# Spreading the change of layer in an attention and two-layer feed-forward kernel: sums asked for earlier, one weight pair split a step sooner, products read ahead of weight work, stores issued by ScalarE

## The chip, the cores and the metric

The kernel runs on one core of a Trainium2 chip. The metric is the device time of one execution in microseconds (us). Three runs of the kernel before gave 1114.27, 1115.67 and 1118.46 us, a median of 1115.67 us. One more execution was profiled; it took 1115.52 us and its span, from the first to the last instruction, is 1113.7 us. All rows below come from that execution.

## What is computed

Attention over 4 batches, 8 heads, 576 positions and head size 64, with a threshold: of each row of scores only those within tau of the row's maximum are kept. Its output, 2304 tokens by 512, goes through two feed-forward layers:

```python
scores = scale * q @ k.T
scores = where(scores >= max(scores) - tau, scores, -1e9)
x = softmax(scores) @ v                       # 2304 x 512 after the heads are put side by side
h = x @ w_in                                  # layer 0: 512 -> 2048
x = (h * tanh(softplus(h))) @ w_out           #          2048 -> 512
out = ((x @ w_a) * (x @ w_b)) @ w_out2        # layer 1: 512 -> 1536, two matrices, -> 512
```

The weights arrive as 64-bit floating point numbers, the rest as 32-bit ones.

## The kernel before

**Stages.** Attention fills the first 280 us. Then the two layers run as one pipeline of 42 steps (`pipeline`, L542). Layer 0 has steps 0 to 23, three passes of eight; layer 1 has steps 24 to 41, three passes of six. A pass covers 768 tokens as two column blocks of 384; a step covers 256 hidden columns. Step 24 is the first of layer 1; the change of layer is the stretch around it.

**Splitting.** Each matrix product is done as three matmuls in a reduced 32-bit form: an operand becomes a high part (a ScalarE copy that rounds, L171 and L282) and a low part (a VectorE subtraction, L172 and L286).

**Seven products.** All passes but the first of layer 0 use a scheme of seven products for a two-by-two block product, in place of eight. It needs sums of input blocks (`prepare`, `sums`, L276: four VectorE subtractions named `t1`, `t2`, `b01`, `t4` by what they write) and sums of weight blocks (`in_weights`, L212). Where a layer 1 step names a weight sum, it is `wsa` or `wsb`, the split weights are `wia` and `wib` (`wii` in layer 0, `woo` and `wop` for the second matrix).

**Gaps.** A product and all that is emitted behind it is a gap: 7 gaps in a layer 0 step, 14 in a layer 1 step (7 for `w_a`, 7 for `w_b`), 8 in the first pass. In each gap the program emits, in this order: the product on TensorE (`product`, L338); whatever earlier gaps had put off to this one (`later`), which includes the sums and splits of the next pass's input; one stage of the weights' conversion (`narrow_some`); the share of weight work (`next(fed)`, L572: sums and splits of a later step's weights); then `after` (L384), which reads the product out of PSUM; last the second matmuls of the step before (`second`, L434). Engines run their instructions in the order in which they are emitted.

**Two banks.** The seven products of a step share PSUM tiles with `bufs=2`, so a product may start only when the reads of the product before it in the same bank are done: product 3 needs the VectorE addition `u2` that reads product 1 (L397), product 5 needs `u3`, the next step's product 1 needs `c12` (L415) of this step's product 6.

**Conversion.** `narrow` (L92) turns 64-bit weights into 32-bit ones in scratch memory: a load of `raw`, four gaps of waiting, then on VectorE L106, L107, L115 and L117 and on ScalarE L105 and L110, then a store (L118). A job is one block of 128 columns; `RATES` says how many jobs start in a gap of each pass of layer 0. SyncE (SP) issues its loads and stores in order, and so it also issues the loads of weights (`load_pair`, L162), of input blocks (L262) and of kept weights (L190).

**Stores between the layers.** `leave` (L460) copies a finished accumulator to `ys` on ScalarE and stores it to `y1d` from SP (L478), four stores of 384 KB in each pass of layer 0.

Of the kernel before, what the change touches and what calls it, by code (L numbers as in the profile page):

```python
# [8 lines left out]
F32 = mybir.dt.float32  # L9
F32R = mybir.dt.float32r  # L10
# [15 lines left out]
NH = 384  # L26
# [5 lines left out]
PRODUCTS = ((0, 0), (4, 1), (1, 2), (5, 3), (3, 4), (2, 5), (6, 6))  # L32
OPENS, CLOSES = (0, 1, 4), (2, 5, 6)
PLAIN, PRE = {("i", 0)}, {"i": 7, "a": 6}
RATES = 0.45, 0.15, 0.4
SCALE = 1.0 / 8.0
BIG = 3.0e38
SEEN = 0.501 / (1.125 * 2.0 ** -15)
# [3 lines left out]
def tile_attn_mish_bilinear(ctx, tc, qd, kd, vd, vd2, tau, w_in, w_out, w_a, w_b, w_out2, out):  # L42
# [49 lines left out]
    def narrow(kind, f):  # L92

        w, block, _ = SOURCES[kind]
        shape, nm = [128, CC, 128], f"{kind}{f}"
        tl = lambda s, dt, bufs: cv.tile(shape, dt, tag="cv" + s, name=s + nm, bufs=bufs)
        raw = cv.tile([128, CC, 256], U32, tag="wraw", name="raw" + nm, bufs=3)
        nc.sync.dma_start(out=raw, in_=block(w, f).bitcast(U32))
        words = raw.rearrange("p c (n t) -> p t c n", t=2)
        hi, lo = words[:, 1], words[:, 0]  # L100
        for _ in range(4):
            yield True
        early = not mish_on
        a, o = tl("a", I32, 2), tl("f", F32, 2)
        A.activation(unit[:, 0::2].rearrange("p (c n) -> p c n", c=CC), lo, AF.Copy, scale=2.0 ** -29)  # L105
        V.tensor_scalar(out=a, in0=hi.bitcast(I32), scalar1=3, scalar2=None, op0=ALU.logical_shift_left)  # L106
        (G if early else V).tensor_tensor(  # L107
            out=a, in0=a, in1=unit.bitcast(I32).rearrange("p (c n) -> p c n", c=CC), op=ALU.add
        )
        A.activation(o.bitcast(I32), hi.bitcast(F32), AF.Copy, scale=SEEN)  # L110
        yield True
        if early:
            A.activation(o, o.bitcast(I32), AF.Sign)
        else:
            V.tensor_scalar(out=o, in0=o.bitcast(I32), scalar1=-1.0, scalar2=1.0, op0=ALU.max, op1=ALU.min)  # L115
# [114 lines left out]
        ] + [lambda: at_gap(now[0] + 2, keep)] * kept  # L230
        return load, items, d

    def out_weights(kind, p, wo):

        d = {}

        def load():
            d["f"] = load_pair(kind, p)

        def start():  # L240
            d["w"] = wo().tile([128, 2, 2, 512], F32R, tag="wo", name=f"wo{kind}{p}_{count['wf']}", bufs=2)
            parts[0][0]()

        parts = [split_items(lambda i=i: (d["w"][:, 0, i], d["w"][:, 1, i]), lambda i=i: d["f"][:, i]) for i in range(2)]
        return load, [start, parts[1][0], parts[0][1], parts[1][1]], d
# [3 lines left out]
    def prepare(layer, s):  # L249

        d = {}
        kinds = ("i", "a")[layer]
        plain, was = (kinds, s) in PLAIN, s and (kinds, s - 1) in PLAIN

        def load():
            for j in range(2):
                for k in range(2):
                    t = raw.tile([128, 2, NH], F32, tag=f"b{j}{k}", name=f"b{j}{k}_{layer}{s}", bufs=1)
                    d[f"b{j}{k}"] = t
                    at_ = 2 * s * NH + k * NH  # L260
                    if layer:
                        nc.sync.dma_start(out=t, in_=y1d[s][:, 2 * j:2 * j + 2, k * NH:(k + 1) * NH])  # L262
                        continue
                    for i in range(2):
                        done = 0
                        while done < NH:
                            b, t0 = divmod(at_ + done, S)
                            n = min(NH - done, S - t0)
                            nc.sync.dma_start(out=t[:, i, done:done + n], in_=xd[2 * j + i][b][:, t0:t0 + n])
                            done += n  # L270

        def sums(k):
            out, x, y = (("t1", "b01", "b00"), ("t2", "b11", "t1"), ("b01", "b11", "b01"), ("t4", "b10", "t2"))[k]
            if out[0] == "t":
                d[out] = raw.tile([128, 2, NH], F32, tag=out, name=f"{out}_{layer}{s}", bufs=1)
            V.tensor_tensor(out=d[out], in0=d[x], in1=d[y], op=ALU.subtract)  # L276

        SRC = ("b00", "t2", "b10", "b01", "t1", "t4", "b11")

        def hi(k):  # L280
            x_now[k] = xp.tile([128, 2, 2, NH], F32R, tag=f"x{k}", name=f"x{k}_{layer}{s}", bufs=1)
            A.activation(x_now[k][:, 0], d[SRC[k]], AF.Copy)  # L282

        def lo(k):
            x = x_now[k]
            V.tensor_tensor(out=x[:, 1], in0=d[SRC[k]], in1=f32(x[:, 0]), op=ALU.subtract)  # L286

        H, L, T = (lambda k: (lambda: hi(k))), (lambda k: (lambda: lo(k))), (lambda k: (lambda: sums(k)))
        if plain:
            places = list(zip((-4, -3, -1, 0) if s else (0, 2, 4, 6), (0, 2, 3, 6)))  # L290
        elif was:
            places = list(zip((-8, -7, -6, -4, -3, -1, 0), (1, 4, 5, 0, 2, 3, 6)))
        else:
            places = [(k - 6, k) for k in range(7)]
        items = [] if plain else [(k - 10, T(k)) for k in range(4)]
        for at_, k in places:
            items += [(at_, H(k)), (at_ + 1, L(k))]
        return load, items

    class Step:  # L300
        pass
# [158 lines left out]
    def leave(st, ps, c, kind):  # L460

        if kind == "c":
            ys[c] = ys_p.tile([128, 2 * NH], F32, tag="ys", name=f"ys{st.i}_{c}", bufs=4)
        y = ys[c]
        end = st.layer and st.s == NS - 1
        dst = y[:, 0:512] if kind == "c" else y[:, 512:768]
        if end and c % 2:
            V.tensor_copy(dst, ps)
        else:
            A.activation(dst, ps, AF.Copy)  # L470
        cols = slice(0, 512) if kind == "c" else slice(512, 768)
        if st.layer:
            t0 = 2 * st.s * NH
            (nc.scalar if end and c % 2 else nc.sync).dma_start(
                out=out[c * 128:(c + 1) * 128, t0 + cols.start:t0 + cols.stop], in_=dst
            )
        elif kind != "c":
            nc.sync.dma_start(out=y1d[st.s][:, c], in_=y)  # L478

    SIX = [("c", 0), ("c", 1), ("d", (0, 1)), ("c", 2), ("c", 3), ("d", (2, 3))]  # L480
    SEVEN = SIX[:5] + [("d", (2,)), ("d", (3,))]
# [14 lines left out]
    for i, st in enumerate(steps):  # L496
        if st.same:
            continue
        if i:
            groups += [(i - 1, "in", kind) for kind in st.kinds]  # L500
        groups.append((i, "out", st.out))
    groups.sort(key=lambda g: (g[0], 1 if g[1] == "out" else 2 * (g[2] == "b")))
    loaded = []

    def load_group():

        if len(loaded) < len(groups):
            i, what, kind = groups[len(loaded)]
            if what == "in":
                load, items, steps[i + 1].w[kind] = in_weights(kind, steps[i + 1].p, steps[i + 1].s)  # L510
            else:
                load, items, steps[i].w[kind] = out_weights(kind, steps[i].p, lambda: wo_p)
            if load:
                load()
            loaded.append(items + [load_group])
# [7 lines left out]

    fed = feed()

    def sizes(k):

        i, what, kind = groups[k]
        return 5 if what == "out" else len(in_weights(kind, steps[i + 1].p, steps[i + 1].s)[1]) + 1

    def background(i):

        n = [0, 0]
        for k, g in enumerate(groups):
# [7 lines left out]
    def pipeline():  # L542
# [4 lines left out]
        for i, st in enumerate(steps):  # L547
# [5 lines left out]
                share = [1] * 6 + spread(early - 6, 2)  # L553
            elif st.gaps < 14 and late:
                share = spread(early, 3) + spread(late, st.gaps - 3)
            if i + 2 < len(steps) and steps[i + 1].last:
                load, rest = prepare(steps[i + 2].layer, steps[i + 2].s)
                load()
                for at_, fn in rest:
                    at_gap(max(steps[i + 2].base + at_, gap), fn)  # L560
            for j, kind in enumerate(st.kinds):
                for k in range(st.gaps // len(st.kinds)):
                    now[0] = gap
# [3 lines left out]
                    if acc_p is not None:  # L567
                        if i == 1 and k == 0:
                            send(len(pairs) - 1)
                        narrow_some(0 if st.last and not st.layer else RATES[st.s] if not st.layer else 0.25)  # L570
                    for _ in range(share[gap - st.base]):
                        next(fed)  # L572
                    after(st, kind, k, gap)
                    for other, what in seconds.pop(gap, ()):
                        second(other, what, gap)
                    gap += 1
# [13 lines left out]
    with late_pools:  # L590
# [208 lines left out]
        def attention():  # L799
# [12 lines left out]
            for n in range(len(units) + 5):  # L812
# [45 lines left out]
                if n == len(units) + 4:  # L858
                    send(len(pairs) - 2)
                if n == 50:  # L860
                    load, rest = prepare(0, 0)
                    load()
                    plan(55, [(2 * k, item) for k, item in rest])
                    load, rest = first_weights(0)
                    load()
# [82 lines left out]
```

## Time and profile before

| what | before |
|---|---|
| median of three runs | 1115.67 us |
| profiled execution | 1115.52 us |
| its span | 1113.7 us |
| TensorE busy | 1092.2 us, 98% |
| VectorE busy | 831.2 us, 75% |
| ScalarE busy | 643.2 us, 58% |
| GpSimd busy | 67.8 us, 6% |
| mean granted TensorE clock | 0.998 |

A share of busy time is a mean over stages. TensorE is what the others have to feed; an engine with 75% over the whole span can be full in one stretch. So each step of the pipeline is held against an undisturbed step of the same form. The names in the profile carry the step's number: `h23i` is a product of step 23 with `w_in`, `h24a` one of step 24 with `w_a`.

### The profile page before, as it was taken

To read this page: it belongs to the slowest core of one execution; us is meant where nothing else is said; L and a number is where in the kernel's file an instruction comes from. 1 tells how busy PE (TensorE), PEld (TensorE's weight loads), DVE (VectorE), ACT (ScalarE), POOL (GpSimd) and SP (SyncE) were. 2 spreads that over 40 slices of the span, in tenths; PEclk is the share of its full clock that TensorE was granted. 3 is DMA by queue.
4 is the path that set the end of the run, shared out by engine and by line. 5 is a ranking of instruction groups with operands and counts; after the bars stand their busy time and mean duration, and the time that the engine had idled before them with its cause. 6 is when DMAs were issued, how large, how long until landed. Compare 5 with 4: busy or idle time off the path is not lost.

```text
span 1113.7 us, 18621 instructions
## 1 busy us (share of the span) xinstructions
PE 1092.2 (98%) x6842; PEld 943.5 (85%) x6842; DVE 831.2 (75%) x1766; ACT 643.2 (58%) x1286; POOL 67.8 (6%) x102
## 2 busy tenths in 40 slices
PE   9999999999999999999999999999999999999998
PEld 7666666666899999999989988889999999999997
DVE  7999999999566787767666697987666666666663
ACT  6889889898665566555655565544343332433321
POOL 1222222222000000000000000000000000000000
PEclk9999999999999999999999999999999999999999
DMA  5556557564666857766387866845414362142401
GB/s 188 147 172 187 166 176 212 181 182 145 187 215 220 274 191 298 255 215 233 124 307 283 309 239 227 275 151 182 168 40 159 113 222 101 38 162 105 167 23 57
DMA packets 77707, 203.14 MB, mean 182 GB/s; under 512 B 6832, under 2 KB 36272, under 8 KB 73776
## 3 DMA queue, kind: packets, MB, share of 16 engines
q1 hardware_dynamic: 74880, 177.01, 47.7%
q10 hardware_dynamic: 2736, 24.94, 5.8%
q8 instruction: 54, 0.88, 0.3%
q14 instruction: 37, 0.30, 0.1%
HBM read 146.01 MB, written 55.91 MB: 181 GB/s over the span
## 4 chain that ended last, share of the span: by engine, by line
PE 74%; DVE 10%; DMA 8%; ACT 5%; issue 2%; SPq 1%; POOL 0%; DVEq 0%; ACTq 0%; POOLq 0%
PE acc L450 22%; PE sums_o L747 6%; PE sp L665 6%; PE tp L728 6%; DMA rawa<-w_a 2%; DMA rawb<-w_b 1%; PE sp L667 1%; DMA rawp<-w_out 1%; ACT ex L685 1%; PE sums_o L751 1%; DMA rawi<-w_in 1%; DVE x L286 1%; DMA inv<-rd 1%; PE warm L632 1%; PE h2i L333 1%
## 5 line engine op out<-in xcount | busy, mean ns | idle before, releaser
L450 PE MATMUL acc<-g,woo 128*128 128x256 f32 (+1 forms) x1152 | 226.6, 339 | 0.0
L450 PEld LDWEIGHTS acc<-g,woo 128*128 128x128 f32 x1152 | 182.1, 189 | 17.0 <-DVE g L376 0.2
L450 PE MATMUL acc<-g,wop 128*128 128x512 f32 (+1 forms) x864 | 170.9, 338 | 1.1 <-ACT g L381 0.7
L450 PEld LDWEIGHTS acc<-g,wop 128*128 128x128 f32 x864 | 137.7, 188 | 14.4 <-ACT g L381 0.9
L692 DVE SCALAR_TENSOR_TENSOR pm<-s,te,ex 128x576 f32<-128x576 f32 x128 | 115.5, 939 | 0.0
L673 DVE TENSOR_SCALAR_CACHE_REDUCE s<-sp 128x576 f32<-128x576 f32 x144 | 103.8, 754 | 15.2 <-PE sp L665 10.5
L685 ACT ACTIVATE ex<-s,m 128x576 f32<-128x576 f32 x144 | 111.1, 784 | 5.1 <-DVE s L673 5.1
L729 ACT ACTIVATE pt<-tp 128x512 f32<-128x512 f32 (+1 forms) x192 | 92.0, 502 | 10.9 <-PE tp L728 7.8
L376 DVE TENSOR_TENSOR g<-hs,g 128x384 fp32r<-128x384 f32 x96 | 51.7, 553 | 52.9 <-ACT g L375 45.5
L728 PEld LDWEIGHTS tp<-ident,pm 128*128 128x128 f32 x576 | 63.9, 141 | 26.0 <-ACT ex L685 15.7
L747 PE MATMUL sums_o<-pt,v 128*64 128x256 f32 x640 | 83.2, 389 | 0.5 <-ACT u L757 0.5
L728 PE MATMUL tp<-ident,pm 128*128 128x128 f32 x576 | 81.2, 279 | 1.8 <-DVE pm L692 1.1
L665 PE MATMUL sp<-k,qs 64*128 64x288 f32 x512 | 80.6, 429 | 0.0
L665 PEld LDWEIGHTS sp<-k,qs 64*128 64x128 f32 x512 | 45.3, 186 | 29.8 <-issue 14.4
L747 PEld LDWEIGHTS sums_o<-pt,v 128*64 128x64 f32 x640 | 40.2, 136 | 25.2 <-issue 6.3
L680 POOL TENSOR_TENSOR te<-m,bar 128x2 f32<-128x2 f32 (+1 forms) x80 | 44.3, 554 | 167.6 <-DVE s L673 164.4
L470 ACT ACTIVATE ys<-acc 128x512 f32<-128x512 f32 (+1 forms) x44 | 20.8, 488 | 33.9 <-PE acc L450 33.9
L381 ACT ACTIVATE g<-s 128x384 fp32r<-128x384 f32 x18 | 9.5, 527 | 42.9 <-DVE s L431 42.7
L171 ACT ACTIVATE woo<-wfo 128x512 fp32r<-128x512 f32 x46 | 27.3, 626 | 10.6 <-PE acc L450 10.6
L172 DVE TENSOR_TENSOR woo<-wfo,woo 128x512 fp32r<-128x512 f32 x46 | 30.7, 684 | 0.0
L381 ACT ACTIVATE g<-c22b 128x384 fp32r<-128x384 f32 x18 | 9.5, 526 | 33.6 <-DVE c22b L431 33.6
L407 DVE TENSOR_TENSOR c22a<-u3a,p5a 128x384 f32<-128x384 f32 x18 | 10.0, 558 | 23.9 <-ACT p5a L405 23.8
(636 smaller groups left out, 2156.7 us busy)
## 6 DMA issues: line engine op xcount, KB each, us to landing
wia<-wpa SPq DMA_DIRECT2D x10, 1792.0 KB
wpi<-wii ACTq DMA_DIRECT2D x7, 1792.0 KB
wii<-wpi SPq DMA_DIRECT2D x7, 1792.0 KB
wfo<-wfo SPq DMA_DIRECT2D x23, 512.0 KB
wpa<-wia ACTq DMA_DIRECT2D x6, 1792.0 KB
v<-vd SPq DMA_DIRECT2D x16, 576.0 KB
rawi<-w_in SPq DMA_DIRECT2D x16, 512.0 KB
rawo<-w_out SPq DMA_DIRECT2D x16, 512.0 KB
```

Source lines behind the costliest of these rows:

```text
L171: lambda: A.activation(dst()[0], src(), AF.Copy),
L172: lambda: V.tensor_tensor(out=dst()[1], in0=src(), in1=f32(dst()[0]), op=ALU.subtract),
L376: at_gap(gap + 1, lambda: V.tensor_tensor(out=gl, in0=hs, in1=f32(gh), op=ALU.subtract))
L450: PE.matmul(ps, w[:, a, f, c * 128:(c + 1) * 128], st.g[f][:, b, cols], start=st.first and f == 0 and m == 0 and (kind == "c" or c % 2 == ...
L665: PE.matmul(sp[:, half, 0:288], d["qs"][r, cols], d["k"][r, keys], start=True, stop=True)
L673: V.tensor_scalar(out=u["s"][:, h].rearrange("p (a c) -> p a c", a=2), in0=u["sp"][h][:, :, 0:288], scalar1=1.0, scalar2=None, op0=ALU.mul ...
L680: G.tensor_tensor(out=u["te"][:, :n], in0=u["m"][:, :n], in1=bar2[:, :n], op=ALU.add)
L685: A.activation(u["e"][:, h], u["s"][:, h], AF.Exp, bias=u["m"][:, h:h + 1], scale=-1.0)
L692: V.scalar_tensor_tensor(out=u["pm"].rearrange("p a c -> p (a c)")[:, h * S:(h + 1) * S], in0=u["s"][:, h], scalar=u["te"][:, h:h + 1], in ...
L728: PE.transpose(tp[:, i], pm[:, j0 + i], ident)
L729: return lambda: A.activation(pt[:, j0:j0 + m], tp[:, :m], AF.Copy)
L747: PE.matmul(po[r], v[0][:, j + 4 * h, r], pair[pi][c & ~1][:, :, j + 4 * h], start=j == 0, stop=j == 4)
```

## The change

- The four loads of input blocks and the four sums of a pass are no longer asked for two steps ahead, in a row (loads together, sums 10 to 7 gaps ahead of the pass), but from up to five steps ahead: loads 30, 28, 26 and 24 gaps ahead, sums 22, 19, 16 and 13. The splits of the input (L282, L286) stay where they were, from 6 gaps ahead.
- The first pair of `w_a` blocks (step 24) is split during step 22 in place of step 23, ahead of that step's `w_out` pair. The first pair of `w_b` counts as early work of step 23.
- In each gap `after` is emitted ahead of the share of weight work.
- A conversion waits five gaps for its `raw` in place of four once the layers run, and the second pass of layer 0 starts 0.2 jobs a gap in place of 0.15.
- ScalarE issues the stores to `y1d`, in place of SP.

```diff
-RATES = 0.45, 0.15, 0.4
+RATES = 0.45, 0.2, 0.4
+LEAD, ASKED, SUMS = 5, (-30, -28, -26, -24), (-22, -19, -16, -13)
+WAIT = 4, 5
...
-        for _ in range(4):
+        for _ in range(WAIT[len(mish_on)]):
             yield True
...
-        items = [] if plain else [(k - 10, T(k)) for k in range(4)]
+        items = [] if plain else [(SUMS[k], T(k)) for k in range(4)]
         for at_, k in places:
             items += [(at_, H(k)), (at_ + 1, L(k))]
-        return load, items
+        loads = [lambda j=j, k=k: load(j, k) for j, k in ((0, 0), (0, 1), (1, 1), (1, 0))]
+        return loads, items
...
-            nc.sync.dma_start(out=y1d[st.s][:, c], in_=y)
+            nc.scalar.dma_start(out=y1d[st.s][:, c], in_=y)
...
-        if i:
-            groups += [(i - 1, "in", kind) for kind in st.kinds]
-        groups.append((i, "out", st.out))
-    groups.sort(key=lambda g: (g[0], 1 if g[1] == "out" else 2 * (g[2] == "b")))
+        for kind in st.kinds:
+            if i:
+                early = st.first and st.layer and kind == "a"
+                groups.append((i - 1 - early, 0.5 if early else 2 * steps[i - 1].layer * (kind == "b"), kind, st))
+        groups.append((i, 1, st.out, st))
+    groups.sort(key=lambda g: g[:2])
...
-            if i + 2 < len(steps) and steps[i + 1].last:
-                load, rest = prepare(steps[i + 2].layer, steps[i + 2].s)
-                load()
-                for at_, fn in rest:
-                    at_gap(max(steps[i + 2].base + at_, gap), fn)
+            if i + LEAD < len(steps) and steps[i + LEAD].first:
+                loads, rest = prepare(steps[i + LEAD].layer, steps[i + LEAD].s)
+                for at_, fn in list(zip(ASKED, loads)) + rest:
+                    at_gap(max(steps[i + LEAD].base + at_, gap), fn)
...
+                    after(st, kind, k, gap)
                     for _ in range(share[gap - st.base]):
                         next(fed)
-                    after(st, kind, k, gap)
```

VectorE in step 22, from the reading of product 3 on. In a row stand the line, the operation, what it writes and what it reads; `ab8` and `fb8` are a conversion job. Before:

```order
L402 TENSOR_TENSOR u3i_22_7524<-h22i1_7469,p1i_22_7461 128x384
L276 TENSOR_TENSOR t1_10_7539<-b01_10_7437,b00_10_7435 128x768
L106 TENSOR_SCALAR ab8_7541<-rawb8_7457 128x512
L107 ISA ab8_7541<-ab8_7541,unit_153 128x1024
L172 TENSOR_TENSOR woo1_40_7506<-wfo1_38_7311,woo1_40_7506 128x512
L276 TENSOR_TENSOR t2_10_7563<-b11_10_7441,t1_10_7539 128x768
L407 TENSOR_TENSOR c22i_22_7550<-u3i_22_7524,p5i_22_7548 128x384
L115 TENSOR_SCALAR fb8_7542<-fb8_7542 128x512
L172 TENSOR_TENSOR woo1_40_7506<-wfo1_38_7311,woo1_40_7506 128x512
L411 TENSOR_TENSOR c21i_22_7568<-h22i1_7469,p1i_22_7461 128x384
L276 TENSOR_TENSOR b01_10_7437<-b11_10_7441,b01_10_7437 128x768
L117 TENSOR_TENSOR fb8_7542<-ab8_7541,fb8_7542 128x512
```

and now:

```order
L403 TENSOR_TENSOR u3i_22_7568<-h22i1_7510,p1i_22_7495 128x384
L214 TENSOR_TENSOR wsa0_24_7502<-wfa0_38_7354,wsa0_24_7502 128x256
L174 TENSOR_TENSOR wia0_23_7501<-wsa0_24_7502,wia0_23_7501 128x512
L119 TENSOR_TENSOR fp8_7546<-ap8_7545,fp8_7546 128x512
L174 TENSOR_TENSOR wia0_23_7501<-wsa0_24_7502,wia0_23_7501 128x512
L408 TENSOR_TENSOR c22i_22_7590<-u3i_22_7568,p5i_22_7588 128x384
L108 TENSOR_SCALAR ap9_7606<-rawp9_7493 128x512
L109 ISA ap9_7606<-ap9_7606,unit_153 128x1024
L412 TENSOR_TENSOR c21i_22_7612<-h22i1_7510,p1i_22_7495 128x384
L117 TENSOR_SCALAR fp9_7607<-fp9_7607 128x512
L416 TENSOR_TENSOR c12i_22_7648<-h22i4_7579,u2i_22_7522 128x384
```

The sums `t1`, `t2` and `b01` are gone from the step (one into step 20, two into step 21), the last, `t4`, stands ahead of step 22's `u2`, and the split of `w_a`'s first pair has come in.

VectorE from the last product of step 26 to `u2` of step 27, both in layer 1. Before:

```order
L415 TENSOR_TENSOR c12b_26_8586<-h26b4_8545,u2b_26_8515 128x384
L431 TENSOR_TENSOR c12b_26_8586<-c12b_26_8586,c12a_26_8480 128x384
L212 TENSOR_TENSOR wsa4_32_8606<-wfa4_51_8456 128x256
L382 TENSOR_TENSOR g1_26_8601<-c22b_26_8557,g1_26_8601 128x384
L382 TENSOR_TENSOR g1_26_8601<-c21b_26_8573,g1_26_8601 128x384
L212 TENSOR_TENSOR wsa4_32_8606<-wsa4_32_8606,wfa4_51_8456 128x256
L172 TENSOR_TENSOR wia4_31_8605<-wfa4_51_8456,wia4_31_8605 128x512
L397 TENSOR_TENSOR u2a_27_8624<-h27a1_8611,p1a_27_8609 128x384
```

and now:

```order
L416 TENSOR_TENSOR c12b_26_8583<-h26b4_8545,u2b_26_8513 128x384
L174 TENSOR_TENSOR wib3_30_8491<-wsb3_31_8492,wib3_30_8491 128x512
L432 TENSOR_TENSOR c12b_26_8583<-c12b_26_8583,c12a_26_8476 128x384
L214 TENSOR_TENSOR wsa4_32_8608<-wfa4_51_8458 128x256
L383 TENSOR_TENSOR g1_26_8601<-c22b_26_8555,g1_26_8601 128x384
L383 TENSOR_TENSOR g1_26_8601<-c21b_26_8571,g1_26_8601 128x384
L398 TENSOR_TENSOR u2a_27_8621<-h27a1_8611,p1a_27_8605 128x384
```

One weight sum and one split of 512 columns that stood ahead of `u2a_27` stand behind it; a split of the `w_b` pair that stood ahead of `c12b_26` has come behind that one.

VectorE from the last product of step 28 to `u2` of step 29, the last step ahead of layer 1's second pass. Before:

```order
L415 TENSOR_TENSOR c12b_28_9038<-h28b4_8997,u2b_28_8967 128x384
L431 TENSOR_TENSOR c12b_28_9038<-c12b_28_9038,c12a_28_8932 128x384
L382 TENSOR_TENSOR g1_28_9053<-c22b_28_9009,g1_28_9053 128x384
L382 TENSOR_TENSOR g1_28_9053<-c21b_28_9025,g1_28_9053 128x384
L397 TENSOR_TENSOR u2a_29_9071<-h29a1_9059,p1a_29_9057 128x384
L382 TENSOR_TENSOR g0_28_8991<-c12b_28_9038,g0_28_8991 128x384
```

and now:

```order
L416 TENSOR_TENSOR c12b_28_9040<-h28b4_9001,u2b_28_8967 128x384
L174 TENSOR_TENSOR wib5_34_8945<-wsb5_35_8946,wib5_34_8945 128x512
L432 TENSOR_TENSOR c12b_28_9040<-c12b_28_9040,c12a_28_8932 128x384
L276 TENSOR_TENSOR t4_11_9071<-b10_11_8896,t2_11_8977 128x768
L383 TENSOR_TENSOR g1_28_9058<-c22b_28_9011,g1_28_9058 128x384
L383 TENSOR_TENSOR g1_28_9058<-c21b_28_9028,g1_28_9058 128x384
L398 TENSOR_TENSOR u2a_29_9076<-h29a1_9064,p1a_29_9062 128x384
L383 TENSOR_TENSOR g0_28_8995<-c12b_28_9040,g0_28_8995 128x384
```

Two instructions have come between `c12b_28` and `u2a_29`: the rest of a weight split and the input sum `t4` of the next pass, 13 gaps ahead of it. Step 35 has the same list.

## Rows read from the trace of the kernel before

**Rows 1.** Stretches: start:end, length, busy us (instructions) by engine, TensorE clock, DMA
```profile
648.56:796.07 147.51, 138.33 (x763) 126.98 (x762) 122.19 (x250) 75.32 (x149) 0.00 (x0) 0.99 0.59 207
632.84:668.58 35.74, 33.45 (x182) 30.28 (x180) 31.41 (x60) 22.41 (x43) 0.00 (x0) 0.95 0.75 272
668.58:722.88 54.30, 49.90 (x277) 45.75 (x277) 46.80 (x96) 31.15 (x63) 0.00 (x0) 1.00 0.72 247
1006.63:1029.80 23.17, 23.17 (x135) 21.94 (x134) 13.96 (x29) 7.42 (x17) 0.00 (x0) 1.00 0.35 126
```

**Rows 2.** TensorE in order of time, first products of steps: start us, length, instruction
```profile
568.63 1.21 PE L352 MATMUL h18i<-x,wii 128*128 128x384 f32 x6
...
585.68 1.20 PE L352 MATMUL h19i<-x,wii 128*128 128x384 f32 x6
...
632.84 1.21 PE L352 MATMUL h22i<-x,wii 128*128 128x384 f32 x6
...
648.56 1.21 PE L352 MATMUL h23i<-x,wii 128*128 128x384 f32 x6
...
796.07 2.39 PE L352 MATMUL h29a<-x,wia 128*128 128x384 f32 x12
```

**Rows 3.** The chain that ended last: start us, us, second matmuls of layer 1
```profile
708.39 1.39 PE acc L450 x6
...
711.87 1.43 PE acc L450 x12
```

**Rows 4.** TensorE in order of time, products that waited: [idle before, releaser]
```profile
656.92 1.51 PE L352 MATMUL h23i<-x,wii 128*128 128x384 f32 x6 [2.25 <-DVE u2i L397]
658.23 2.76 PE L450 MATMUL acc<-g,woo 128*128 128x512 f32 x6
...
662.08 1.55 PE L450 MATMUL acc<-g,woo 128*128 128x512 f32 x6
...
676.14 1.33 PE L352 MATMUL h24a<-x,wia 128*128 128x384 f32 x6 [1.06 <-DVE u2a L397]
...
703.55 1.33 PE L352 MATMUL h25a<-x,wia 128*128 128x384 f32 x6 [1.37 <-DVE u2a L397]
...
776.78 1.33 PE L352 MATMUL h28a<-x,wia 128*128 128x384 f32 x6 [0.18 <-DVE u2a L397]
...
824.15 1.33 PE L352 MATMUL h30a<-x,wia 128*128 128x384 f32 x6 [0.54 <-DVE u2a L397]
```

**Rows 5.** VectorE by line and form, 400 to 760 us: busy us, mean ns, idle before
```profile
L376 DVE TENSOR_TENSOR g<-hs,g 128x384 fp32r<-128x384 f32 x68 | 36.1, 552 | 25.6 <-ACT g L375 25.6
L172 DVE TENSOR_TENSOR woo<-wfo,woo 128x512 fp32r<-128x512 f32 x32 | 21.2, 684 | 0.0
...
L276 DVE TENSOR_TENSOR t<-b,t 128x768 f32<-128x768 f32 x5 | 4.8, 951 | 0.0
...
L212 DVE TENSOR_TENSOR wsa<-wfa 128x256 f32<-128x256 f32 x10 | 4.2, 417 | 0.0
```

**Rows 6.** VectorE in order of time, in step 25
```profile
700.37 0.55 DVE L382 TENSOR_TENSOR g<-c21b,g 128x384 fp32r<-128x384 f32 x1
700.84 0.42 DVE L106 TENSOR_SCALAR aa<-rawa 128x512 int32<-128x512 int32 x1
```

**Rows 7.** Waits of SP's queue, 520 to 580 us: total us, times, longest
```profile
SPq L478 <- ACT ys L470: 30.5, 2, 26.6
SPq L118 <- DVE fp L117: 13.7, 2, 10.7
```

**Rows 8.** VectorE in order of time, steps 17 and 18
```profile
570.19 0.43 DVE L106 TENSOR_SCALAR ab<-rawb 128x512 int32<-128x512 int32 x1 [4.67 <-DMA rawb<-w_b]
...
571.68 0.55 DVE L415 TENSOR_TENSOR c12i<-h17i,u2i 128x384 f32<-128x384 f32 x1
```

**Rows 9.** TensorE in order of time, step 18
```profile
572.29 1.31 PE L352 MATMUL h18i<-x,wii 128*128 128x384 f32 x6 [1.06 <-DVE c12i L415]
```

**Rows 10.** DMA issues of ScalarE, line 218: ns least/median/most, first and last start
```profile
L218 ACTq DMA_DIRECT2D wpi<-wii x7: 326/326/340, 410.6 to 500.1; - x7
```

More of the change, by code (lines that the diff above doesn't have):

```diff
@@ L231, in in_weights, with out_weights @@
         return load, items, d
-    def out_weights(kind, p, wo):
+    def out_weights(kind, p):
         d = {}
@@ L240, in start @@
         def start():
-            d["w"] = wo().tile([128, 2, 2, 512], F32R, tag="wo", name=f"wo{kind}{p}_{count['wf']}", bufs=2)
+            d["w"] = wo_p.tile([128, 2, 2, 512], F32R, tag="wo", name=f"wo{kind}{p}_{count['wf']}", bufs=2)
             parts[0][0]()
@@ L253, in prepare, with load @@
         plain, was = (kinds, s) in PLAIN, s and (kinds, s - 1) in PLAIN
[L255 to L270, printed above, removed]
+        def load(j, k):
+            t = raw.tile([128, 2, NH], F32, tag=f"b{j}{k}", name=f"b{j}{k}_{layer}{s}", bufs=1)
+            d[f"b{j}{k}"] = t
+            at_ = 2 * s * NH + k * NH
+            if layer:
+                nc.sync.dma_start(out=t, in_=y1d[s][:, 2 * j:2 * j + 2, k * NH:(k + 1) * NH])
+                return
+            for i in range(2):
+                done = 0
+                while done < NH:
+                    b, t0 = divmod(at_ + done, S)
+                    n = min(NH - done, S - t0)
+                    nc.sync.dma_start(out=t[:, i, done:done + n], in_=xd[2 * j + i][b][:, t0:t0 + n])
+                    done += n
         def sums(k):
@@ L498, in tile_attn_mish_bilinear, with weights @@
             continue
-        if i:
-            groups += [(i - 1, "in", kind) for kind in st.kinds]
-        groups.append((i, "out", st.out))
-    groups.sort(key=lambda g: (g[0], 1 if g[1] == "out" else 2 * (g[2] == "b")))
+        for kind in st.kinds:
[4 more added lines that the diff above has]
+    groups.sort(key=lambda g: g[:2])
     loaded = []
+    def weights(g):
+        _, order, kind, st = g
+        return out_weights(kind, st.p) if order == 1 else in_weights(kind, st.p, st.s)
     def load_group():
         if len(loaded) < len(groups):
[L508 to L512, printed above, removed]
+            g = groups[len(loaded)]
+            load, items, g[3].w[g[2]] = weights(g)
             if load:
@@ L524, in tile_attn_mish_bilinear @@
     fed = feed()
-    def sizes(k):
-        i, what, kind = groups[k]
-        return 5 if what == "out" else len(in_weights(kind, steps[i + 1].p, steps[i + 1].s)[1]) + 1
     def background(i):
@@ L535, in background @@
             if g[0] == i:
-                n[g[2] == "b"] += len(loaded[k]) if k < len(loaded) else sizes(k)
+                n[g[1] == 2] += len(loaded[k]) if k < len(loaded) else len(weights(g)[1]) + 1
         return n
@@ L860, in attention @@
                 if n == 50:
-                    load, rest = prepare(0, 0)
-                    load()
+                    loads, rest = prepare(0, 0)
+                    for load in loads:
+                        load()
                     plan(55, [(2 * k, item) for k, item in rest])
```

## The prediction

> **What bounds the kernel now.** I read the busy shares first: TensorE is busy 98% of the span, so all that can be won is what it loses in places. Then TensorE in order of time, to find them: I noted where the first product of each step starts and compared steps of one form. Step 22 of layer 0 takes 632.84 to 648.56, 15.72 us [rows 2]; a layer 1 step takes 23.17 us, with TensorE busy throughout and VectorE for 13.96 us of it [rows 1]. Held against these, steps 23 to 28 are slow. They last from 648.56 to 796.07, 147.51 us [rows 1, 2]. Undisturbed they are 15.72 + 5 x 23.17 = 131.57, plus the second matmuls that step 24 takes over from the layer 0 form (1.39 and 1.43) less those of half the last size that run on into step 29 (0.71, half of 1.43) [rows 3]: 133.68. **13.83 us are lost there.** The first row of the same table splits them: TensorE idle 147.51 - 138.33 = 9.18; the clock, whose mean there is 0.99; and the rest about the stalls, since a product starts slower after one.
>
> The clock: behind the 2.25 us stall in step 23, six second matmuls took 2.76 us where the next six took 1.55 [rows 4], and the stretch's mean clock is 0.95 [rows 1]. The granted clock stood at its lower level, 1.2 GHz in place of 2.4, for part of it; about 1.6 us are lost by it, 1.21 of them in those six. No other stall listed, all of 1.4 us or less, has that behind it.
>
> What ends the stalls: in step 23 and later it is VectorE, by `u2` [rows 4]. VectorE is full there: 31.41 of 35.74 us in steps 22 and 23 and 46.80 of 54.30 in steps 24 and 25 [rows 1], and it runs one queue in order, so a late item delays all behind it.
>
> One more place, by the same comparison: step 18 lasts 568.63 to 585.68, 17.05 in place of 15.72, 1.33 us lost [rows 2]. A wait of 1.06 us for `c12i` stands in it [rows 9]; `c12i` stood behind a conversion that waited 4.67 us for `rawb` [rows 8]; and SP had held its queue for 26.6 us at a `y1d` store until ScalarE had written `ys` [rows 7], with the `raw` loads behind it.
>
> **The change part by part.** Durations of VectorE: 0.95 us for an input sum or split of 768 columns, 0.68 for a weight split of 512, 0.55 for 384 columns, 0.42 for a weight sum of 256 [rows 5]. In a full queue starts are closer by about 0.08: 0.47 from one 0.55 instruction to the next [rows 6]. With such distances, and the lists of instructions before and now, I count VectorE's work between one `u2` and a later one.
>
> *From `u2` of step 22 to that of step 24*, two steps of 15.72, 31.4 us of TensorE: before 35.8 us of VectorE, now 32.2. Three of the four input sums have left (3 x 0.87 = 2.6), about half a conversion too (1.0); the earlier `w_a` pair moves from step 23 into 22, so that step 22 has 14.2 (before 16.9) and step 23 18.0 (before 18.9). Before, VectorE came into step 23 late already; now it comes on time and falls behind by 2.3 only in the course of it. `u3` and `c12` have more than 3 us from the end of their product to the one that waits for them (another product and two groups of second matmuls, 1.39 each [rows 3], stand between), so I expect no stall in step 23. Its whole loss comes back: 35.74 - 2 x 15.72 = 4.30, the clock's part included.
>
> *Step 24.* Ahead of `u2a_24` stand, behind `c12i_23`, the same input splits as before and two `woo` splits (1.21) in place of a weight sum and a `wia` split (0.94). By the same count VectorE reaches `c12i_23` some 2.0 us late, against 2.4 before. The stall was 1.06 [rows 4]; I take 0.9.
>
> *Steps 24 to 26, from the middle of 24 to the middle of 26*, 46.3 us of TensorE: before 46.3 us of VectorE, so each wait that VectorE itself has goes to TensorE at full price; now 40.4, since three conversions of 2.0 us are done earlier by the higher rate. What stays is uneven: 12.1 in the second half of 24 and 11.6 in the first half of 25, each against 11.6. Ahead of `u2a_25` stand a split, a conversion's product and a weight sum (0.68, 0.68, 0.42) where the list of step 28, which stalls for 0.18 [rows 4], has a split and two sums (0.68, 0.42, 0.42): 0.45 before any lag, and with the 0.5 that the second half of 24 leaves over, about 0.9. `u3a_25` may cost another 0.5. So 1.4 in step 25, where 1.37 is one of its two stalls before. In steps 26 to 28 a weight sum and a split have gone behind `u2a` and a split has come ahead, 0.42 less: the 0.18 goes.
>
> *What stays of the 13.83.* Stalls of 0.9 + 1.4 = 2.3. A us of stall cost (13.83 - 1.6) / 9.18 = 1.33 us, so 3.1. Back come 10.7.
>
> *New stalls.* In steps 28 and 34 the sums of the next pass stand in the second half, 11.4 us of VectorE against 11.6 (8.5 before). Ahead of `u2a_29` stand now a split and `t4` (0.68 + 0.95 = 1.63), against 1.52 for step 28's list before: 0.18 + 0.11, and a little lag, about 0.4. Ends: nothing, if VectorE stands idle at `c12b`, and 1.1 (twice step 30's 0.54 [rows 4], for a lag on top). 0.4 x 1.33 x 2 steps = 1.1 lost. Steps 30 and 36 keep their input splits in the same gaps: no change.
>
> *Stores from ScalarE.* The copy before each store is ScalarE's own, so no other engine is waited for. An issue takes it 0.33 us [rows 10], 12 of them 3.9 us in three places. ScalarE is busy 22.41 of 35.74 and 31.15 of 54.30 [rows 1]; its room hides them. If it didn't, 3.9 would be the price; below nothing is possible too, since SP's waits go: up to 1.33 in step 18. With the fifth gap of waiting as well I take 1.3. Of the Trainium skill, the page "DMA: Bandwidth & Descriptors", section "Issuing engines are not separate DMA queues", says that issuing from several engines only saves the time it takes to issue; by it this edit would be worth nothing on the path, and the sum 1.3 less. The wait of 26.6 us in SP's queue [rows 7] speaks for more: what is freed is the loads behind a store that waits.
>
> *Loads and sums earlier, the fifth gap, the higher rate.* Loads of the same size, spread. Steps 9 to 15 take the conversions and the third pass's sums: at most 14.2 us of VectorE in a step of 15.7, so hidden. If a block came later than its sum, VectorE would wait in order; the ends are nothing and the 1.33 of step 18 for each.
>
> **Sum.** From the profiled execution's 1115.52 (0.15 under the median, so either serves): -10.7 + 1.1 - 1.3 = -10.9, 1104.6. The count leaves out waits of VectorE for ScalarE and for loads, so I give 0.4 back: **1105.0 us**.
>
> **Rivals.**
>
> *The lag comes back by another wait.* VectorE's splits need ScalarE's copy first, and conversions their loads; if such waits eat the 5.9 us of room in 24 to 26, only step 23's loss comes back, 1115.5 - 4.3 = 1111.2. For it: full VectorE in [rows 1] has idle time of its own. Against: the loads are spread and SP no longer stands at the stores.
>
> *All of it comes back.* If `u2` ahead of weight work does more than the count says, the whole 13.83 and 1.33 go, and some of steps 30 and 36: 1115.5 - 15.2 - 1 = 1099.3. Against: the same two splits stand ahead of `u2a_30`.
>
> *The change does not do it.* If TensorE's lost time lay in the products themselves and not in the emptying, all would stay at 1115. Against: [rows 4] names VectorE at each stall.
>
> *Slower: input blocks later than their sums.* A sum is asked for 6 gaps behind its last load, 13.5 us in layer 0 (6 x 15.72 / 7) and 9.9 in layer 1. SP can stand 10.7 us at a conversion's store [rows 7], with the load behind it, and a load like `rawb` was 4.67 us late after such a hold [rows 8], at 1.33 us of TensorE, so that some 3.3 us of lateness are absorbed. A block 7.6 us late would cost 4.3. There are five passes with four loads each; from four such blocks on it outweighs the gain and the bound below, with one in each pass the time is 1115.5 - 10.9 + 21.5 = 1126. Against: each load now has its own gap, and DMA in the bad stretch is busy 0.6 to 0.75 [rows 1].
>
> **How the numbers follow.** What a measurement of this kernel can tell from no change is about 0.5%, 5.6 us: under 1110.1 is faster, over 1121.3 slower. My forecast has 0.62, with its own range of 1101 to 1109; the lag's return 0.17 (1109 to 1115, a fifth of it faster); all comes back 0.10; no effect 0.05; slower 0.06. Faster: 0.62 + 0.10 + 0.03 = 0.75; same 0.14 + 0.05 = 0.19; slower 0.06. The range for 8 in 10 leaves out the slower case, no effect, the top of the lag's return and the bottom of all comes back: 1099 to 1113.
>
> **What would show it.** No wait for `u2i` in step 23 and a mean clock of 1.00 there; steps 23 to 28 in 134 to 140 us; a stall of 0.5 to 1.2 at `u2a_24`, stalls at `u2a_25`, and none at 26 to 28; a new one at `u2a_29` and `u2a_35`, steps 30 and 36 as before; step 18 at 15.7 and no wait of SP for `ys` in layer 0. Wrong: VectorE waiting for loads of `b` or `raw`, or the stalls of steps 24 to 26 still there with ScalarE named before VectorE.

## The result and the profile after

The changed kernel took 1102.66 us, the median of 5 runs (1102.39 to 1103.64); the kernel before, over the 5 runs beside them, 1115.67. The ratio is 0.988 with a 95% interval of 0.9864 to 0.9896: 1.2% faster, more than the 0.5% that can be told from no change. 1105.0 was predicted, in a range of 1099 to 1113. The profiled execution's span is 1100.6 us (before 1113.7), TensorE is busy for 1087.8 us of it and VectorE for 826.9.

The same three stretches by engine, cut at the first products of steps 23 and 29, 22 and 24, and 24 and 26, of the changed kernel (columns as in [rows 1]):

```profile
643.66:781.85 138.19, 135.70 (x763) 125.77 (x762) 113.32 (x232) 68.75 (x136) 0.00 (x0) 1.00 0.55 197
627.95:659.50 31.55, 31.55 (x181) 29.16 (x179) 28.91 (x58) 22.84 (x44) 0.00 (x0) 1.00 0.74 269
659.50:711.98 52.48, 49.99 (x278) 45.65 (x277) 44.29 (x92) 28.36 (x57) 0.00 (x0) 1.00 0.68 236
```

Steps 23 to 28 last 138.19 us in place of 147.51 [rows 1], TensorE idle there 2.49 in place of 9.18. Steps 22 and 23 last 31.55 against 31.44 undisturbed, at full clock: VectorE still works 28.91 us there, but nobody waits for it. The products that still waited, in order of time; these are the rows that answer to [rows 4]:

```profile
666.59 1.34 PE L353 MATMUL h24a<-x,wia 128*128 128x384 f32 x6 [0.85 <-DVE u2a L398]
...
679.95 1.31 PE L353 MATMUL h24b<-x,wib 128*128 128x384 f32 x6 [0.17 <-DVE u2b L398]
...
688.71 1.33 PE L353 MATMUL h25a<-x,wia 128*128 128x384 f32 x6 [1.02 <-DVE c12b L416]
...
692.12 1.32 PE L353 MATMUL h25a<-x,wia 128*128 128x384 f32 x6 [0.32 <-DVE u2a L398]
...
786.26 1.33 PE L353 MATMUL h29a<-x,wia 128*128 128x384 f32 x6 [0.27 <-DVE u2a L398]
...
810.48 1.33 PE L353 MATMUL h30a<-x,wia 128*128 128x384 f32 x6 [0.52 <-DVE u2a L398]
```

The 2.25 us stall of step 23 is gone, those of 26 to 28 too, and a new one stands in step 29 (and its like in step 35). Step 18, which answers to [rows 2] and [rows 9], has no wait and takes 15.71 us from its first product to the next step's:

```profile
565.07 1.20 PE L353 MATMUL h18i<-x,wii 128*128 128x384 f32 x6
...
580.78 1.21 PE L353 MATMUL h19i<-x,wii 128*128 128x384 f32 x6
```

Where the 13.1 us of span came from, by step times (first product to first product, both traces):

| steps | before minus after |
|---|---|
| 23 to 28 | 9.32 |
| 18 | 1.34 |
| 1, 5, 7, 8, 9, 15 | 0.53, 0.35, 0.07, 0.73, 0.87, 0.72: 3.27 |
| 29 and 35 | -0.54, -0.52 |
| start of step 0 | 0.29 |

### The profile page after: what moved, and what is told of

It is laid out like the page before. It is cut to its first block, busy times and chain, and to the rows that moved or that the text cites. A ratio compares the mean times of both kernels' runs of the same rounds, so it can differ in the third digit from the quotient of the medians.

```text
span 1100.6 us, 18610 instructions
## 1 busy us (share of the span) xinstructions
PE 1087.8 (99%) x6842; PEld 942.6 (86%) x6842; DVE 826.9 (75%) x1766; ACT 644.5 (59%) x1286; POOL 67.8 (6%) x102
## 4 chain that ended last, share of the span: by engine, by line
PE 91%; DVE 5%; ACT 3%; issue 1%; ACTq 0%; POOL 0%; DVEq 0%; POOLq 0%
PE acc L451 30%; PE sums_o L746 6%; PE sp L664 6%; PE tp L727 6%; PE sp L666 1%; PE sums_o L750 1%; ACT ex L684 1%; PE h0i L334 1%; PE h6i L334 1%; PE h4i L334 1%; PE h7i L334 1%; PE h3i L334 1%; PE h5i L334 1%; PE h2i L334 1%; PE h1i L334 1%
## 5 line engine op out<-in xcount | busy, mean ns | idle before, releaser
L672 DVE TENSOR_SCALAR_CACHE_REDUCE s<-sp 128x576 f32<-128x576 f32 x144 | 103.7, 753 | 14.8 <-PE sp L664 10.1
```

The costliest lines, as they stand in the source:

```text
L672: V.tensor_scalar(out=u["s"][:, h].rearrange("p (a c) -> p a c", a=2), in0=u["sp"][h][:, :, 0:288], scalar1=1.0, scalar2=None, op0=ALU.mul ...
```

## The experiments

The theory is the prediction's: VectorE's queue runs in order, and what stands in it ahead of `u2`, `c12` and `c21` sets TensorE's stalls; it can be counted from the lists. The rival: loads that come late, for SP's or for DMA's sake. Step times are compared between profiles, since attention's end alone, which none of the edits touches, lies between 282.4 and 285.0 us in them. A step's time runs from its first product to the first product of the next step, so a wait ahead of a step's first product counts in the step before. The medians come from other executions than the profiles and, in three groups (e1 to e4, e5 to e8, e9 to e12), from three chips; those of e2, e3, e4, e5 and e10 lie 0.6 to 2.3 us further from 1102.66 than the step times account for. Intervals are those of the ratio to the kernel before.

**e1: SP issues the stores again.**

```diff
-            nc.scalar.dma_start(out=y1d[st.s][:, c], in_=y)
+            nc.sync.dma_start(out=y1d[st.s][:, c], in_=y)
```

> The changed kernel with the y1d stores issued by SP again. Theory (VectorE's full queue at the change of layer sets most of the gain, the stores only the loads behind them in SP's queue): steps 23 to 28 stay at about 138 us; step 18 goes back from 15.7 to as much as 17.0, and steps 8, 9 and 15, which had lost 0.7 to 0.9 each before, may lose that again: 1104 to 1106 against 1102.7. Rival (the gain is mostly SP no longer standing at the stores, so that loads come in time everywhere): steps 23 to 28 go back by 4 us or more too, 1108 to 1112.

1102.31 us, ratio 0.9876 (0.9847 to 0.9905). Every step as in the changed kernel, 18 too; 24 is 0.56 shorter. SP's queue, 510 to 570 us (total, times, longest), of this kernel:

```profile
SPq L479 <- ACT ys L471: 23.1, 2, 19.8
```

SP stands at the store for 19.8 us again, and nobody is late for it. Nor did the change free SP: in the same stretch of the changed kernel it stands as long at a conversion's own store, which waits for VectorE, and nobody is late there either:

```profile
SPq L120 <- DVE fb L119: 32.1, 2, 20.7
```

Both sides of the expectation fail: in the changed kernel it is worth nothing that ScalarE issues the stores.

**e2: loads and sums as before.**

```diff
-LEAD, ASKED, SUMS = 5, (-30, -28, -26, -24), (-22, -19, -16, -13)
+LEAD, ASKED, SUMS = 2, (-30, -30, -30, -30), (-10, -9, -8, -7)
```

> The changed kernel with input loads and sums where they were before (loads together two steps ahead, sums 10 to 7 gaps ahead). Theory (counting VectorE's work between its readings): step 23 loses some 0.5 us and step 24 about 1.5 more than in the changed kernel, while the new stalls at u2a_29 and u2a_35 (0.27 and 0.26) go: net +0.5 to +1.5, 1103 to 1104. Rival (the sums in step 22 are what filled VectorE, as their 3.5 us there suggest): the 2.25 us stall in step 23 with its slow clock returns, +3 to +5, 1106 to 1108.

1104.79 us, ratio 0.9896 (0.9867 to 0.9925). By step times against the changed kernel: 9 +0.33, 23 +1.54, 24 +0.72, 29 -0.53, 35 -0.57, so +1.5 in these, the top of what the theory has; the median is 0.8 above its range. Of step 23's 1.54 a part belongs to step 24: it is this wait, ahead of step 24's first product.

```profile
663.04 1.33 PE L353 MATMUL h24a<-x,wia 128*128 128x384 f32 x6 [0.54 <-DVE c21i L412]
```

In step 23 itself `u2i` is waited for again, but for 0.34 us and not for 2.25, at a full clock: the rival falls. The early sums are worth 2.3 us at the change of layer and give 1.1 back.

**e3: the first `w_a` pair in step 23 again.**

```diff
-                early = st.first and st.layer and kind == "a"
+                early = 0
```

> The changed kernel with the first w_a pair split during step 23 again. Theory (count): VectorE gets some 4 us more work in step 23, so c21, c12 and u2 hold steps 24: three stalls of about 1.0, 1.1 and 1.6 in place of one of 0.85, +2.9 us of stall, +3.5 to +4.5 in all, 1106 to 1107. Rival (late loads set the stalls): no change within 1 us, 1102 to 1104.

1110.03 us, ratio 0.994 (0.9921 to 0.996). Steps 23 +2.10 and 24 +2.96. The stalls in order of time:

```profile
655.82 1.32 PE L353 MATMUL h23i<-x,wii 128*128 128x384 f32 x6 [0.73 <-DVE u3i L403]
...
662.06 1.33 PE L353 MATMUL h24a<-x,wia 128*128 128x384 f32 x6 [1.05 <-DVE c21i L412]
...
665.72 1.31 PE L353 MATMUL h24a<-x,wia 128*128 128x384 f32 x6 [0.94 <-DVE c12i L416]
...
671.24 1.33 PE L353 MATMUL h24a<-x,wia 128*128 128x384 f32 x6 [1.48 <-DVE u2a L398]
```

The three stalls counted as 1.0, 1.1 and 1.6 are there, with one more, the first. So the time is above the expected 1106 to 1107: 5.1 us by step times where 3.5 to 4.5 were expected. The rival, late loads, falls. The pair a step sooner is the largest single part: 5.1 us.

**e4: weight work ahead of the reading.**

```diff
-                    after(st, kind, k, gap)
                     for _ in range(share[gap - st.base]):
                         next(fed)
+                    after(st, kind, k, gap)
```

> The changed kernel with the share of weight work emitted ahead of the reading of the product, as before. Theory (count): stalls of 0.2 come back at u2a of 26, 27 and 28, step 24's shrinks by 0.25, those at 29 and 35 shrink or go: about the same, 1102 to 1104. Rival (reading products first is what keeps TensorE fed): two splits (1.2 us) stand ahead of u2 in every step from 22 to 28, 1.2 us more stall where there was one and 0.5 to 1 where there was none: 1106 to 1110.

1106.93 us, ratio 0.9924 (0.9899 to 0.9948). Step 9 +1.09, 23 -0.12, 24 +1.65, 25 +0.51, 26 to 28 +0.32 each, 29 and 35 -0.49 each: +3.1 in these. The count is right for 26 to 28 (stalls of 0.16 to 0.18) and for 29 and 35, and wrong for 24, whose stall grew where it was to shrink:

```profile
668.81 1.31 PE L353 MATMUL h24a<-x,wia 128*128 128x384 f32 x6 [1.09 <-DVE u2a L398]
```

The 0.25 counts what stands between `c12i_23` and `u2a_24` alone (1.21 against 0.94). The two `woo` splits that left this place stand ahead of `c12i_23` now, and VectorE works from 649 us to `u2a_24` with no break over 0.14 us: `c12i_23` starts 2.14 us behind step 24's first product in place of 1.33, and `u2a_24` 7.01 us behind it in place of 6.48. The time is within the rival's range, which named 0.5 to 1 us in every step; in 26 to 28 it was 0.3.

**e5: four gaps of waiting in the changed kernel.**

```diff
-WAIT = 4, 5
+WAIT = 4, 4
```

> The changed kernel with four gaps of waiting between a conversion's load and its use, as before. Theory now (after the stores turned out to be worth nothing: the fifth gap is what ended the waits for raw): VectorE and ScalarE wait for raw again, some of the 1.3 of step 18 and of the 0.5 to 0.9 of steps 1, 8, 9 and 15 come back: +1.5 to +3.5, 1104 to 1106. Rival (the order of reads and the spread sums freed those steps): steps 1 to 18 stay, within 0.7 us, 1102 to 1103.4.

1107.55 us, ratio 0.9934 (0.9914 to 0.9954). Steps 1 +1.75, 5 +0.89, 24 +1.92, with 23 and 25 0.45 shorter together; 8, 9, 15 and 18 stay undisturbed. The median is 1.6 above the expected range. In step 24 ScalarE, in order of time:

```profile
686.99 0.78 ACT L107 ACTIVATE unit<-rawb 128x512 int16<-128x512 uint32 x1 [3.97 <-DMA rawb<-w_b]
687.63 0.64 ACT L112 ACTIVATE fb<-rawb 128x512 int32<-128x512 f32 x1
688.18 0.47 ACT L406 ACTIVATE p5b<-h24b 128x384 f32<-128x384 f32 x1
```

and TensorE:

```profile
688.71 1.59 PE L353 MATMUL h24b<-x,wib 128*128 128x384 f32 x5 [1.85 <-ACT p5b L406]
```

A conversion that comes to its `raw` before the load has landed holds ScalarE for 3.97 us, and the reading of a product stands behind it. The waits come back as expected, but in other places than the steps named.

**e6: the kernel before with the fifth gap alone.**

```diff
-        for _ in range(4):
+        for _ in range(5 if mish_on else 4):
             yield True
```

> The kernel before with the fifth gap alone. Theory now: step 18 falls from 17.05 to 15.7, some of steps 1, 8, 9 and 15 too, and steps 23 to 28 stay at 146 to 148: -1.5 to -4, 1112 to 1114. Rival (the freed loads need the stores or the spread as well): step 18 stays at 17, 1115 to 1116.

1111.73 us, ratio 0.9969 (0.9953 to 0.9984). Against the kernel before: steps 1 -0.53, 5 -0.35, 8 -0.73, 9 -0.85, 15 -0.72, 18 -1.33: 4.5 us, and 23 to 28 stay at 147.97. The medians on the one chip (1114.75 for the kernel before) differ by 3.0. The waits for `raw` from 280 to 640 us (total, times, longest), before:

```profile
ACT unit L105 <- DMA rawb<-w_b: 9.6, 3, 3.9
DVE ab L106 <- DMA rawb<-w_b: 8.5, 3, 4.7
ACT unit L105 <- DMA rawo<-w_out: 8.2, 3, 3.9
ACT unit L105 <- DMA rawa<-w_a: 8.1, 3, 4.8
ACT unit L105 <- DMA rawi<-w_in: 7.7, 4, 2.8
DVE ao L106 <- DMA rawo<-w_out: 3.4, 2, 1.8
ACT unit L105 <- DMA rawp<-w_out: 3.3, 1, 3.3
DVE aa L106 <- DMA rawa<-w_a: 2.8, 1, 2.8
DVE ai L106 <- DMA rawi<-w_in: 1.4, 2, 1.1
DVE ap L106 <- DMA rawp<-w_out: 1.2, 2, 1.0
```

and with five gaps:

```profile
ACT unit L105 <- DMA rawo<-w_out: 1.4, 1, 1.4
ACT unit L105 <- DMA rawp<-w_out: 1.2, 1, 1.2
ACT unit L105 <- DMA rawa<-w_a: 1.1, 1, 1.1
```

They fall from 54.2 us to 3.7. This one number frees the steps ahead of the change of layer: without it (e5) the waits are back, without the stores (e1) they are not.

**e7: the kernel before with ScalarE's stores alone.**

```diff
-            nc.sync.dma_start(out=y1d[st.s][:, c], in_=y)
+            nc.scalar.dma_start(out=y1d[st.s][:, c], in_=y)
```

> The kernel before with the stores issued by ScalarE alone. The prediction's reason (SP's wait of 26.6 us delays rawb): step 18 falls to 15.7, -1.3, 1114.3. Rival, the skill's rule: nothing, 1115 to 1116, and step 18 stays at 17 because the loads of raw come too late for four gaps anyway.

1117.39 us, ratio 1.0017 (1.0003 to 1.0032): no gain. Step 18 does fall by 1.33, as predicted; steps 9 and 14 grow by 1.74 and 0.92, and over all steps that differ the sum is zero. In step 9, ScalarE in order of time:

```profile
438.16 0.78 ACT L105 ACTIVATE unit<-rawa 128x512 int16<-128x512 uint32 x1 [6.24 <-DMA rawa<-w_a]
```

The loads are asked for at other times, and another one comes too late. The stores move the lateness; they do not end it.

**e8: two late places moved behind `u2`.** `t4` 12 gaps ahead of the pass in place of 13, the low parts of the last two input splits two gaps later.

```diff
-LEAD, ASKED, SUMS = 5, (-30, -28, -26, -24), (-22, -19, -16, -13)
+LEAD, ASKED, SUMS = 5, (-30, -28, -26, -24), (-22, -19, -16, -12)
...
-            items += [(at_, H(k)), (at_ + 1, L(k))]
+            items += [(at_, H(k)), (at_ + (1 if plain or at_ < -1 else 3), L(k))]
```

> The changed kernel with t4 one gap later (12 gaps ahead, behind u2a of steps 29 and 35) and the low parts of the last two input splits two gaps later (behind u2a of steps 24, 30 and 36). Theory (what stands ahead of u2 in VectorE's queue sets the stall): the stalls at u2a_24 (0.85), 29, 30, 35 and 36 (0.27, 0.52, 0.26, 0.54) go: steps 24 -1, 29 and 35 -0.5, 30 and 36 -1.0 each, -4 in all, 1098 to 1099.5. Rival (the sums of VectorE's work in the half steps set it, wherever an item stands): the stalls move to u3 or c21, 1102 to 1103.

1100.69 us, ratio 0.9874 (0.9855 to 0.9892). Steps 24 -0.45, 29 -0.53, 30 -0.81, 35 -0.53, 36 -0.81: 3.1 of the 4 expected; 8 and 9 are 0.50 longer together, which leaves 2.6. The stalls at `u2` of 24, 29, 30, 35 and 36 are gone; ahead of step 25's first product one of 0.54 for `c21b` has come, which is why step 24 gains only 0.45. What stands ahead of `u2` sets the stall: the rival falls but for that one place.

**e9 and e11: the changed kernel and e8's once more, beside each other.**

> The changed kernel once more, beside the three that follow, for a comparison on one chip: 1102 to 1104.

> The kernel with late splits once more, beside the changed kernel: 2.0 to 3.5 us faster than it, as the step times of its first profile say (24 -0.45, 29 and 35 -0.5 each, 30 and 36 -0.8 each).

On one chip the changed kernel took 1103.79 us (ratio 0.9889, 0.9867 to 0.9911) and the late splits 1099.60 (0.9851, 0.9827 to 0.9876), 4.2 us less. By step times it is 2.8 (24 -0.55, 29 and 35 -0.55 each, 30 and 36 -0.81 each, against +0.51 in 8 and 9): within the 2.0 to 3.5 expected, which the medians exceed. The two intervals overlap, while the runs of the late splits (1099.25 to 1099.84) all lie under all runs of the changed kernel there (1101.91 and more). TensorE's waits in the layers, late splits (total, times, longest):

```profile
PE h25a L353 <- DVE c12b L416: 1.0, 1, 1.0
...
PE h25a L353 <- DVE c21b L412: 0.4, 1, 0.4
...
PE h25a L353 <- DVE u2a L398: 0.3, 1, 0.3
PE h24b L353 <- DVE u2b L398: 0.2, 1, 0.2
```

**e10: 0.15 conversions a gap in the second pass.**

```diff
-RATES = 0.45, 0.2, 0.4
+RATES = 0.45, 0.15, 0.4
```

> The changed kernel with the second pass of layer 0 at 0.15 conversions a gap, as before. Theory (count): three conversions of 2.0 us of VectorE go back into steps 24 to 26; one more stall, of about 1.35 at u2a_26, +2 us, 1104 to 1106. Rival (three conversions fit in VectorE's room there): within 0.7 us of the changed kernel, stalls only where it has them.

1107.11 us, ratio 0.9923 (0.9898 to 0.9948). Steps 25 +0.29 and 26 +2.46, by

```profile
716.58 1.31 PE L353 MATMUL h26a<-x,wia 128*128 128x384 f32 x6 [0.69 <-DVE c12b L416]
...
720.89 1.33 PE L353 MATMUL h26a<-x,wia 128*128 128x384 f32 x6 [1.24 <-DVE u2a L398]
```

where the count had one stall of 1.35 at `u2a_26`; the median is 1.1 above the expected range. Four conversions start behind step 24's first product in the changed kernel, seven here: three fewer are worth 2.8 us.

**e12: all conversions done before step 24**, on top of e8.

```diff
-RATES = 0.45, 0.2, 0.4
+RATES = 0.45, 0.2, 0.5
```

> The late splits and 0.5 conversions a gap in the third pass of layer 0 in place of 0.4, so that all conversions are done before step 24. Theory (count): VectorE's work from the middle of 24 to the middle of 26 falls by another 6 us, the stalls in 24 and 25 (2.0 us listed in the late splits' profile, 3.5 us of step time) go, steps 16 to 23 stay at 15.7 although they take more (up to 15.4 us of VectorE): 1097 to 1098. Rival (the loads of raw at this rate come too late, as before the fifth gap): waits for raw in steps 16 to 23, 1099 to 1103.

1109.64 us, ratio 0.9943 (0.9921 to 0.9965). Steps 23 to 28 fall to 133.89, within 0.2 us of undisturbed, and TensorE has no wait in them: the count is right there. But 17 and 21 are 5.1 and 5.4 longer, 18 to 20 1.3 together, and the time lies above both ranges. ScalarE and TensorE in step 17:

```profile
566.20 0.66 ACT L112 ACTIVATE fa<-rawa 128x512 int32<-128x512 f32 x1 [5.33 <-DMA wfp<-fp]
566.76 0.48 ACT L406 ACTIVATE p5i<-h17i 128x384 f32<-128x384 f32 x1
```

```profile
567.29 1.57 PE L353 MATMUL h17i<-x,wii 128*128 128x384 f32 x6 [2.92 <-ACT p5i L406]
```

Not `raw` is late, as the rival had it, but the buffer that a job writes, of which there are two: the store two jobs back had not left it. That store was issued at 555.39, and the buffer came free 10.8 us later. The DMA engines are busy all of 551 to 566 us, but so they are in e11, where no product waits; what slowed the store was not separated. The wait stands ahead of a reading again. A third buffer was not tried.

## Why the prediction was right, and where not

The main step held: VectorE's full queue at the change of layer set the loss. With less VectorE work there the stalls go, to none in e12, and with more of it, or with it in worse places, they come back (e2, e3, e4, e10). Step 23's loss came back whole (4.30 predicted, 4.18 measured, 20.02 to 15.84), with the slow clock. Step 24's stall: 0.9 predicted, 0.85 measured at `u2a_24`, and 0.17 in its second half. Step 25's: 1.4 predicted, 1.02 + 0.32 measured. Steps 26 to 28: none, none. Steps 29 and 35: 1.1 lost predicted, 1.06 measured. Steps 30 and 36: no change, as predicted.

In step 25 the sum agrees by luck. The prediction had 0.9 at `u2a_25` and perhaps 0.5 at `u3a_25`; measured are 0.32 at `u2a_25` and 1.02 at `c12b`, which the count did not price. A wait for `c12b` was there before, and so was one for ScalarE in step 24. [rows 4] shows neither: that VectorE ends each stall holds for the rows shown there and not for all stalls.

```profile
694.51 1.34 PE L352 MATMUL h24b<-x,wib 128*128 128x384 f32 x6 [0.67 <-ACT p5b L405]
699.11 1.31 PE L352 MATMUL h25a<-x,wia 128*128 128x384 f32 x6 [1.29 <-DVE c12b L415]
```

- *What stays of the 13.83*: mis-sized. 3.1 predicted, 4.51 measured (138.19 - 133.68). The listed stalls of steps 23 to 28, 2.36, are close to the 2.3 of the prediction, but a us of stall cost 1.9 us of step time and not 1.33. Waits too short for the list do not make this up: all idle time of TensorE there is 2.49. A price per us was the wrong form. Each stall takes 0.1 to 0.4 us on top of its idle time, the short ones too: 2.14 us of idle in two stalls of step 26 went with 2.67 of step time (before against now), 0.18 in step 27 with 0.32, 0.27 in step 29 with 0.55, 0.52 in step 30 with 0.81 (e8), 1.02 in two stalls of step 24 with 1.82 (e12). So stalls that grow shorter cost more for each us. 9.32 came back, not 10.7.
- *The clock's part*: the 1.6 us were taken as a loss of their own, and e6 speaks against that. It has the same stall in step 23 at a full clock, and its step 23 is only 0.28 shorter, with VectorE busy for 19.30 of 19.74 us and further waits for it (0.47 for `u3i`; 0.60 for `c21i` ahead of step 24); steps 23 to 28 last 147.97 there and 147.51 before. The fifth gap differs too, so e6 does not show this by itself.
- *Stores from ScalarE*: the step that failed. Its 1.3 us did come, but not by the stores: without them step 18 is undisturbed too (e1), and alone they gain nothing (e7). That the term came out right is luck: the fifth gap, in the same change, gives it. The rule that was cited against the edit, of the Trainium skill ("DMA: Bandwidth & Descriptors", "Issuing engines are not separate DMA queues"), agrees with the ratio of e1 to within its interval: issuing from another engine was worth nothing. SP's wait of 26.6 us [rows 7] was read as the cause of the late `rawb`. It was one, since step 18 is free without these stores (e7); but the load, issued at 559.78, also took 10.4 us to land [rows 8], longer than four gaps (9.0), and one in step 9 took 10.1. The other twelve loads for which ScalarE waited between 280 and 640 us landed 4.1 to 7.6 us after their issue, within four gaps (8.4 in the first pass): they were issued too late. One of these, for step 5, stood behind a conversion's own store, at which SP had waited 4.1 us for VectorE; the last row below is the issue of the late `rawb`:

```profile
360.80 0.32 SPq L118 DMA_DIRECT2D wfi<-fi  x1
361.17 1.53 SPq L98 DMA_DIRECT2D rawo<-w_out  x2
...
365.77 0.79 ACT L105 ACTIVATE unit<-rawo 128x512 int16<-128x512 uint32 x1 [3.88 <-DMA rawo<-w_out]
...
559.78 0.49 SPq L98 DMA_DIRECT2D rawb<-w_b  x1
```

So it was right that SP's queue delays loads, and wrong that taking the `y1d` stores out of it ends that. What held each of the twelve was not separated.

- *The fifth gap*: counted at nothing of its own, beside the stores. Alone it is worth 4.5 us by step times (e6). It gives a load one gap more, and it also moves each conversion's store a gap back in SP's queue; which of the two helps was not separated. In the changed kernel steps 18 and 1 to 15 give back the same 1.34 and 3.27; of the 3.27 the prediction had nothing, since it compared only step 18 and the steps around the change of layer with an undisturbed one. Step 18's row [rows 8] named the wait for `rawb`, and the list of waits in e6 names the others. In the changed kernel some of it is doubly secured: with four gaps 8, 9, 15 and 18 stay free and 1, 5 and 24 suffer (e5).

The errors cancel in part: 1.4 too much at the change of layer, 3.3 too little before it, 0.4 held in reserve. Together they make the 2.3 us by which the prediction was too high.

What each part is worth, taken out of the changed kernel, by step times: pair a step sooner 5.1, fifth gap about 4.5 (steps 1, 5, 24, less 0.5 in 23 and 25: 4.1 by e5), reading first 3.1, higher rate 2.8, early sums 1.5 net, stores 0. They add up to 17.0, more than the gain of 13.1, so some of them cover for others.

## What to carry to other kernels

Where an engine's queue is full and in order, compare what stands ahead of the instruction that others wait for, list against list, and not only its busy share; moving two items behind a reading (e8) gained 2.6 us, more than asking for the loads and sums of a pass steps earlier (e2, 1.5). Price a stall as its idle time and an addition for each stall (0.1 to 0.4 us here), not by the us alone. Compare every step with an undisturbed one before pricing a change, and read all waits of one kind together before giving them a cause: most of the late loads were issued too late, two took too long, and one more gap between load and use covered nearly all of them. A queue that stood still for 20 us cost nothing here (e1), because what was behind it was asked for early enough.

## What the runs showed of the hardware

The lower clock after a stall is not decided by the stall's length alone. In the kernel before, 2.25 us of idle TensorE in step 23 went with a granted clock of 0.95 over steps 22 and 23 [rows 1, 4]; e6 has nearly the same stall, 2.24 us, and its step 23 ran at full clock:

```profile
643.43:663.17 19.74, 16.43 (x91) 14.36 (x89) 19.30 (x39) 14.68 (x28) 0.00 (x0) 1.00 0.53 190
```

e5's stall of 1.85 us went with 0.91 over 680 to 700 us:

```profile
680.00:700.00 20.00, 17.57 (x88) 15.95 (x87) 16.75 (x37) 10.69 (x23) 0.00 (x0) 0.91 0.69 237
```

What tells them apart, the runs do not show.
